# A new listed order of steps, with the rotating buffers given out by the list, in an attention and Mish kernel on one core

## The chip, the cores and the metric

The kernel runs on one core of one Trainium2 chip. The metric is the device time of one execution in microseconds (us): 923.94, the median of 3 runs, which lay between 922.16 and 925.21.

## What is computed

Eight batches of eight heads, 576 tokens each, of width 64: scores, a causal mask (a band of 32 keys for heads 0 to 3, every fourth of the last 128 keys for heads 4 to 7), a softmax and the product with v. The result, 4608 tokens of width 512, goes through a feed-forward network of 2048 channels with the Mish activation.

```python
scores = scale * np.matmul(q, k.transpose(0, 1, 3, 2))
mask_plain = (rel >= 0) & (rel < window)                  # window 32, dilation 4
mask_dil = (rel >= 0) & (rel < window * dilation) & (rel % dilation == 0)
scores = np.where(masks[None, :, :, :], scores, -1000000000.0)
scores = scores - np.max(scores, axis=-1, keepdims=True)
attn = np.exp(scores)
attn = attn / (np.sum(attn, axis=-1, keepdims=True) + 1e-09)
x = np.matmul(attn, v)                                    # then [4608, 512]
h = x @ w_in
sp = np.where(h > 20.0, h, np.log1p(np.exp(np.minimum(h, 20.0))))
out = (h * np.tanh(sp)) @ w_out
```

The two weights come as float64 and are unpacked on the chip.

## The kernel before, in words

**Units.** The work is cut into 16 units of 288 tokens (half a batch each). Units 0 to 3 do attention in float32, and turn x by products on TensorE. Units 4 to 7 use float16, and DMA transposes. Units 8 to 15 go in pairs 4 to 7; a pair's first layer is made by seven products per chunk of the channels, Strassen's way (`za` to `zg`, all products on L921), from sums of x (`zt`) and of the weights (`wf`, on POOL, L855 to L861), which lie in DRAM and are streamed in (`zl`, L879).

**Steps.** Each function of a unit is a generator in a few pieces, and each piece is a step with a two-letter name: `wl`, `wm`, `ww`, `ws`, `wp` load, measure, decode (DVE L394 to L397), scale and split a piece of the weights (ACT L351, ACT L406, DVE L409); `ld`, `lv` load q, k and v; `pr` prepares them (POOL L536 makes the low half of q); `sp` is the scores' product (PE L609, with the mask from PE L606 in units 0 to 3), `sc` reads them out of the bank (DVE L633, from unit 4 on), finds the maximum (DVE L639) and subtracts it (DVE L641); `ex` is the exponential (ACT L680; in the first units L667, straight from the bank), `tp` turns it (DVE L724, then the DMA of L727), `va` multiplies by v (PE L763; L757 in units 0 to 3), `ff` is a product of the first layer (PE L1009) and its Mish (ACT L1012; L931 for pairs), `gt` cuts Mish's result into float16 halves (ACT L1024, DVE L1026), `fo` is a product of the second layer (PE L1036), whose result ACT L1050 writes to a tile y that L1052 sends to DRAM, and `kw` is a number of products of zeros (`keep_warm`, PE L1065), whose results nobody reads.

**Order.** A text, `ORDER` (L40 to L179), lists all pieces of all units, 1 name for each piece. The loop at the end of the kernel goes through it and calls the next piece of the generator that is named. So the text sets the order of the instructions on every engine and every queue; nothing else does. What stands behind `=` in a name is the number of the buffer that the step is given:

```python
            name, _, at = name.partition("=")
            place[:] = [int(at)] if at else []
```

```python
        turns[name] = place[0] if place else (turns.get(name, -1) + 1) % len(tiles)
```

**Banks.** All products write to four PSUM tiles, `b0` to `b3` of 2 x 512 float32. A product for a bank waits until the engine that reads the bank's last result has read it. `keep_warm` is given `banks[3:]`, that is b3 alone.

**Rotating buffers.** In the kernel before, the raw weights (`raw`, 4 buffers), the transposed exponentials (`pp`, 2), `xs` (2), the scores (`sb`, 4), the results (`y`, 2) and Mish's results (`hm`, 3) are tiles of a pool with `bufs=N`: the pool gives them out in turn. `hm` is asked for in the same piece as the product that Mish will read (L1009, L921).

Of the kernel before, what the change touches and what calls it, by code (L numbers as in the profile page):

```python
# [10 lines left out]
F16 = mybir.dt.float16  # L11
BF16 = mybir.dt.bfloat16
F32 = mybir.dt.float32
# [39 lines left out]
tx1.0 tx1.0 tx1.3=0 va1.2 tx1.3 wp0.1.0 kw9=0 tx1.1=2 tx1.1 tx1.1 kw3=0 tx1.2=1 sp2.3=3 tx1.2 tx1.3 tx1.3 wl1.3.0
wl1.2.0 ww0.2.0 tx1.2 pr2=2 pr2 tx1.2 wm1.3.0 ww1.3.0 sc2.3 gt0.0=1 wp0.2.0 gt0.0 fs1 ff1.0=0 ww1.3.0 wl1.3.1 wm1.3.1
ff1.0 ff1.1=1 ff1.1 wp0.2.0 ff1.2=2 ff1.0 ff1.1 ff1.2 wl1.2.1 gt1.0=2 ff1.3=0 ff1.2 ww1.3.1 sp2.1=1 ld3 lv3 ww1.3.1
ex2.3 ws1.3=2 ff1.3 ws1.3 sc2.1 tp2.3=2 tp2.3 gt0.3 ff0.2=3 ff0.2 wm1.2.0 gt1.0 wm1.2.1 ff0.3=2 ex2.1 ff0.3 ww1.2.0
ff1.6=1 ww1.2.0 ff0.2 ff0.3 ff1.6 gt0.1=3 ww1.2.1 ww1.2.1 ff1.6 ff1.3 ws1.2=2 gt0.1 ff0.4=3 gt1.1=4 ff0.4 wp1.3.0
va2.3=1 tp2.1=0 tp2.1 ws1.2 ff0.4 sp3.0=2 gt1.1 sp3.1=0 va2.3 wp1.3.0 wp1.2.1 ff1.7=3 va2.3 wl1.0.1 ff1.7 wp1.2.1
ff1.4=1 ff1.7 gt1.3=5 sc3.0 wl1.0.0 wp1.2.0 sc3.1 gt1.3 ff1.5=3 wp1.3.1 ff1.4 ff1.5 sp3.3=2 va2.1=0 wp1.2.0 ff1.4
wm1.0.1 wp1.3.1 wl1.1.0 ff1.5 gt1.2=6 gt1.2 ff0.5=1 ww1.0.1 ff0.5 wm1.0.0 va2.1 fo1.2.0=3 ff0.5 ww1.0.0 gt0.2=7  # L60
ww1.0.0 fo1.2.1 fo1.2.2 ex3.1 va2.1 ws1.0=1 gt0.2 tp3.1=0 fo1.2.3 tp3.1 ws1.0 wm1.1.0 tp2.0=0 sp3.2=1 tp2.0 fo1.2.3
sp2.2=0 sc3.3 fo1.2.3 fo1.3.0 ld4 sc3.2 ex3.3 fo1.3.1 ww1.1.0 lv4 ww1.1.0 fo1.3.2 ex3.2 fo1.3.3 sc2.2 fo0.2.0=2 ex2.2
pr3 fo0.2.1 ww1.0.1 fo0.2.2 fo1.3.3 fs2 fo0.2.3 fo0.2.3 xa2.1=4 tx2.3=1 va2.0=0 fo0.2.3 tx2.3 tp2.2=3 fo0.3.0 fo1.3.3
tp2.2 va2.0 wp1.0.0 tx2.3 fo0.3.1 va2.0 wp1.0.0 ex3.0 fo0.3.2 fo0.3.3 fo0.3.3 wl1.1.1 xa2.0=0 fo0.3.3 tx2.0=3 va2.2=1
# [124 lines left out]
QB = 96  # L189
# [4 lines left out]
def attn_mish_ffn_kernel(  # L194
# [12 lines left out]
    P = 128  # L207
# [916 lines left out]
```

## Time and profile before

| | |
|---|---|
| median of the runs | 923.94 us |
| profiled execution, span | 926.8 us |
| mean granted clock of TensorE in it | 0.985 of full speed |
| TensorE products (PE) | 898.3 us busy, 97% |
| weight loads (PEld) | 725.8 us, 78% |
| VectorE (DVE) | 656.0 us, 71% |
| ScalarE (ACT) | 584.6 us, 63% |
| GpSimd (POOL) | 176.1 us, 19% |

The profile has one execution, from its first to its last instruction; its span is 2.9 us over the median of the runs. A row of a timeline says when a stretch of equal instructions began, how long it took, and in brackets how long the engine stood idle before it and what ended that. A row of the windows says how long each engine was busy in a stretch, and which clock TensorE was granted (1.00 is 2.4 GHz).

### The profile page before, as it was taken

How to read it: one execution, taken by the hardware profiler on the slowest of the kernel's cores; microseconds unless marked ns; L12 is line 12 of the kernel's file. 1: busy time of each engine (PE TensorE's matmuls, PEld its weight loads, DVE VectorE, ACT ScalarE, POOL GpSimd, SP SyncE). 2: the span in 40 equal slices, each digit the busy share in tenths (PEclk: the TensorE clock that was granted, in tenths of full speed). 3: DMA queues.
4: the chain of work that ended last, by engine and by line, in shares of the span. 5: the costliest groups of instructions: out<-in, count | busy, mean ns of one | idle time of the engine just before them, and what ended most of it. 6: DMA issues, size and time to landing. Idle time of an engine off the chain costs nothing.

```text
span 926.8 us, 21709 instructions
## 1 busy us (share of the span) xinstructions
PE 898.3 (97%) x9194; PEld 725.8 (78%) x9197; DVE 656.0 (71%) x905; ACT 584.6 (63%) x832; POOL 176.1 (19%) x196
## 2 busy tenths in 40 slices
PE   8899999999999989999889899999999999999998
PEld 7788888887787868887667777777877788887776
DVE  5787996678888687888868986997479965333400
ACT  2658775665685755768747677667687667535521
POOL 1000031114201160412430512131023500220000
PEclk9889999999999999999989999999999999999999
DMA  7844444130554365543656877865548655544300
GB/s 252 247 123 137 141 138 146 44 111 17 155 88 96 81 161 122 126 126 77 143 146 140 160 182 215 190 153 115 179 104 207 119 172 174 94 112 144 114 27 26
DMA packets 194194, 122.80 MB, mean 132 GB/s; under 512 B 139088, under 2 KB 182832, under 8 KB 194096
## 3 DMA queue, kind: packets, MB, share of 16 engines
q1 hardware_dynamic: 194096, 121.41, 50.9%
q8 instruction: 72, 1.18, 0.5%
q14 instruction: 26, 0.21, 0.1%
HBM read 78.38 MB, written 16.78 MB: 103 GB/s over the span
## 4 chain that ended last, share of the span: by engine, by line
PE 75%; DVE 10%; ACT 5%; DMA 4%; SPq 2%; issue 2%; POOL 2%; ACTq 0%; DVEq 0%
PE b L1036 30%; PE b L921 17%; PE b L1009 16%; PE b L609 3%; PE b L763 2%; PE b L757 2%; PE b L1065 2%; DVE sb L633 1%; DVE nm L639 1%; DVE k L539 1%; DMA raw<-in_w_in 1%; DVE g L1026 1%; DVE sb L641 1%; PE b L734 1%; DVE p L724 1%
## 5 line engine op out<-in xcount | busy, mean ns | idle before, releaser
L1036 PE MATMUL b<-g,w 128*128 128x288 f16 x3072 | 392.3, 288 | 0.0
L1036 PEld LDWEIGHTS <-w 128*128 128x128 f16 x3072 | 298.8, 98 | 77.0 <-issue 0.2
L1009 PE MATMUL b<-xf,w 128*128 128x288 f16 x1536 | 195.4, 287 | 1.6 <-ACT hm L1012 1.0
L1009 PEld LDWEIGHTS <-w 128*128 128x128 f16 x1536 | 149.7, 98 | 41.1 <-issue 2.1
L921 PEld LDWEIGHTS <-w 128*128 128x128 f16 x1344 | 130.9, 98 | 36.3 <-issue 2.9
L1026 DVE SCALAR_TENSOR_TENSOR g<-hm,sg,g 128x1152 f16<-128x1152 f32 x64 | 94.4, 1481 | 67.8 <-ACT g L1024 67.8
L921 PE MATMUL b<-xf,w 128*128 128x288 f16 x960 | 138.7, 286 | 2.9 <-ACT y L1050 1.5
L1050 ACT ACTIVATE y<-b,fo 128x288 f32<-128x288 f32 x60 | 43.3, 721 | 116.4 <-PE b L1036 93.7
L536 POOL TENSOR_TENSOR q<-qn,q 128x288 f16<-128x288 f32 (+1 forms) x36 | 55.6, 1573 | 158.1 <-ACT q L529 158.1
L1024 ACT ACTIVATE g<-hm,sg 128x1152 f16<-128x1152 f32 x64 | 80.3, 1254 | 2.6 <-PE b L1036 1.0
L1012 ACT ACTIVATE hm<-b,fs 128x576 f32<-128x576 f32 x64 | 45.9, 738 | 40.4 <-PE b L1009 24.9
L680 ACT ACTIVATE sb<-sb,ln_p 96x704 f32<-96x704 f32 (+3 forms) x48 | 42.5, 888 | 32.2 <-DVE sb L641 32.0
L931 ACT ACTIVATE hm<-hm,fs 128x576 f32<-128x576 f32 x48 | 36.4, 772 | 35.7 <-DVE hm L966 15.9
L724 DVE TENSOR_TENSOR p<-sb,p 96x704 f16<-96x704 f32 (+3 forms) x48 | 48.4, 1017 | 7.1 <-ACT p L722 6.9
L641 DVE TENSOR_TENSOR sb<-sb,nm 96x512 f32<-96x512 f32 (+4 forms) x60 | 50.9, 849 | 2.1
L639 DVE TENSOR_REDUCE nm<-sb 96x4 f32<-96x512 f32 (+4 forms) x60 | 44.9, 748 | 1.7
L855 POOL TENSOR_TENSOR hm<-w 128x1024 f32<-128x1024 f16 x8 | 18.8, 2353 | 139.5 <-DVE g L1026 139.5
L921 PE MATMUL b<-w,w 128*128 128x288 f16 x192 | 42.9, 286 | 0.0
L609 PE MATMUL b<-k,q 64*96 64x128 f16 (+3 forms) x1008 | 31.9, 210 | 8.5 <-POOL q L536 2.6
L609 PEld LDWEIGHTS <-q 64*72 64x72 f16 (+1 forms) x1008 | 26.8, 116 | 16.7 <-issue 10.1
L722 ACT CAST p<-sb 96x704 f16<-96x704 f32 (+3 forms) x48 | 37.8, 789 | 1.4 <-DMA pT<-p 0.3
L763 PEld LDWEIGHTS <-pT 128*128 128x128 f16 (+3 forms) x1008 | 35.4, 98 | 3.6 <-issue 1.7
(180 smaller groups left out, 1159.8 us busy)
## 6 DMA issues: line engine op xcount, KB each, us to landing
w<-wd SPq DMA_DIRECT2D x56, 512.0 KB
qn<-in_qT SPq DMA_DIRECT2D x16, 576.0 KB
out_T<-y SPq DMA_DIRECT2D x64, 144.0 KB
raw<-in_w_in SPq DMA_DIRECT2D x16, 512.0 KB
raw<-in_w_out SPq DMA_DIRECT2D x16, 512.0 KB
vn<-in_v SPq DMA_DIRECT2D x48, 128.0 KB
wd<-hm SPq DMA_DIRECT2D x32, 128.0 KB
knd<-in_kdT SPq DMA_DIRECT2D x16, 208.0 KB
```

Source lines behind the costliest of these rows:

```text
L536: nc.gpsimd.tensor_tensor(lo, x, hi, op=ALU.subtract)
L609: nc.tensor.matmul(o, q, k, start=start, stop=stop, skip_group_check=True)
L639: nc.vector.tensor_reduce(nm[:nq, :, j:j + n], x, axis=AX.X, op=ALU.max, negate=True)
L641: nc.vector.tensor_tensor(blocked(sb, c0, n, w), x, nm[:nq, :, j:j + n].unsqueeze(3).broadcast_to([nq, 2, n, w]), op=ALU.add)
L724: nc.vector.tensor_tensor(lo, src, hi, op=ALU.subtract)
L763: nc.tensor.matmul(avv[:, h, j], pp[:nk, c:c + P], vv[vi][:nk, j, hh, :], start=(i == 0), stop=(i == 2))
L921: nc.tensor.matmul(o[:, h, :HT], t[:, c, wi, h * P:(h + 1) * P], form_of(p, x, c, xi), skip_group_check=True, start=start and n == 0, stop ...
L1009: nc.tensor.matmul(ph[:, h, :HT], w1[j][c // WIDE][:, c % WIDE, wi, k * P:(k + 1) * P], x_of(d, xi, c), start=(n == 0), stop=(n == len(seq ...
L1012: nc.scalar.activation(d["m"][j][:, k0:k0 + 2], ph[:, :, :HT], AF.Mish, scale=d["fs"][:, j:j + 1])
L1024: nc.scalar.activation(g[:, 0], m, AF.Identity, scale=sg)
L1026: nc.vector.scalar_tensor_tensor(g[:, 1], m, sg, g[:, 0], ALU.mult, ALU.subtract)
L1036: nc.tensor.matmul(po[:, :HT], w2[:, e, j, wi, k * P:(k + 1) * P], d["g"][j][:, gi, k, :], start=(j == 0 and n == 0), stop=(j == NCH - 1 a ...
```

## The change

It replaces the list of the order by another with the same steps, except for the products of zeros: 251 for 451. All 251 are listed ahead of the first product of the first layer. In the list before, 375 are, 12 follow soon after, and 64 are spread over the rest of the list: 1, 30, 15, 15 and 3 at five places from unit 6's second layer on. `raw`, `pp`, `xs`, `sb`, `y` and `hm` become fixed lists of tiles, and the order's number says which one a step gets. `pp` is taken a piece later, and `hm` is taken in the piece that first writes it. `keep_warm` may use any of the four banks. The instructions are otherwise the same in number on each engine, but for ScalarE's loads of a function table: 52 for 40. Lines move by 7 or 8: L609, L1009, L1012, L1036 and L1050 become L616, L1017, L1020, L1044 and L1058.

```diff
 ORDER = """
...
-pr10 ld11 sp10.0=3 sc10.0 sp10.1=0 sp10.2=3 sc10.2 ex10.0 sc10.1 ex10.1 pr11 pr11 tp10.1=0 tp10.1 tp10.0=1 tp10.0
...
+pr10 va8.3 ff7.0=1 sp10.0=2 sc10.0=1 sp10.2=3 sp10.1=1 fo6.3.3=1 ex9.2 tp9.2=1 tp9.2 fo6.0.0=0 fo6.0.1 ex10.0 va9.3=2
...
+    raw4 = [early.tile([P, WIDE, CH], I64, name=f"raw{i}") for i in range(4)]
+    pps = [early.tile([P, 2, HT], F32, name=f"pp{i}") for i in range(2)]
+    xss = [early.tile([QB, 4, P], F32, name=f"xs{i}") for i in range(2)]
+    sbs = [pool.tile([QB, 2, NR * KD], F32, name=f"sb{i}") for i in range(4)]
+    ys = [pool.tile([P, HT], F32, name=f"y{i}") for i in range(2)]
...
-        t = early.tile([P, WIDE, CH], I64, name="raw", bufs=4)
+        t = take("raw", raw4)
...
-        sb = None if by_pe else pool.tile([QB, 2, NR * KD], F32, name="sb", bufs=4)
+        sb = None if by_pe else take("sb", sbs)
...
-        pp = d["p", pair] = early.tile([P, 2, HT], F32, name="pp", bufs=2)
-        yield
+        yield
+        pp = d["p", pair] = take("pp", pps)
...
+    hms = [pool.tile([P, FPC, HT], F32, name=f"hm{i}") for i in range(3)]
...
-            m[j] = pool.tile([P, FPC, HT], F32, name="hm", bufs=3)
+            m[j] = take("hm", hms)
...
         y = V[p]["Y", j] = take("b", banks)
+        product(p, j, "11", "11", y, True, False)
+        yield
         m = hm_of(2 * p, j)
-        product(p, j, "11", "11", y, True, False)
-        yield
...
-        if j not in d["m"]:
-            d["m"][j] = pool.tile([P, FPC, HT], F32, name="hm", bufs=3)
...
-        nc.scalar.activation(d["m"][j][:, k0:k0 + 2], ph[:, :, :HT], AF.Mish, scale=d["fs"][:, j:j + 1])
+        nc.scalar.activation(hm_of(u, j)[:, k0:k0 + 2], ph[:, :, :HT], AF.Mish, scale=d["fs"][:, j:j + 1])
...
-            y = pool.tile([P, HT], F32, name="y", bufs=2)
+            y = take("y", ys)
...
-        warm = take("w", banks[3:])
+        warm = take("w", banks)
```

Three places of the order follow, first of the kernel before, then of the change. The first is ScalarE at the start: the decoding of the first weights (L351), their split (L406) and the first exponentials of unit 0, read out of the banks (L667). `w` is a weight, `sb` the scores' tile.

```order
L351 ACTIVATE w100_104<-raw_159 128x1024
L272 ACTIVATE m_fb_96<-m_f_81 96x352
L406 ACTIVATE w100_104<-raw_159,ws1_330 128x2x512
L406 ACTIVATE w101_105<-raw_152,ws1_330 128x2x512
L351 ACTIVATE w130_110<-raw_418 128x1024
L667 ACTIVATE sb_430<-b1_73 72x2x288
L667 ACTIVATE sb_447<-b0_72 96x2x352
```

```order
L358 ACTIVATE w101_119<-raw1_77 128x1024
L279 ACTIVATE m_fb_110<-m_f_95 96x352
L358 ACTIVATE w130_124<-raw2_78 128x1024
L674 ACTIVATE sb0_84<-b0_72 96x2x352
L674 ACTIVATE sb1_85<-b1_73 96x2x352
L413 ACTIVATE w101_119<-raw1_77,ws1_398 128x2x512
L413 ACTIVATE w100_118<-raw0_76,ws1_398 128x2x512
```

The third decoding and the first two exponentials stand ahead of the split of the first weights now, not behind it. On SyncE's queue the load of the third piece of the weights stands ahead of the loads of v, not behind them.

The second place is TensorE at the first scores of unit 10 (behind each row shown follow more of its kind, each with its weight load).

```order
L1036 MATMUL b1_73<-g3_141,w2_112 128x288
...
L609 MATMUL b3_75<-k2_6350,q2_6348 96x128
...
L609 MATMUL b0_72<-k2_6350,q2_6348 96x128
...
L609 MATMUL b3_75<-k2_6350,q2_6348 72x72
...
L1009 MATMUL b2_74<-xf0_119,w100_104 128x288
```

```order
L1044 MATMUL b0_72<-g2_157,w2_126 128x288
...
L616 MATMUL b2_74<-k2_6146,q2_5988 96x128
...
L616 MATMUL b3_75<-k2_6146,q2_5988 72x72
...
L616 MATMUL b1_73<-k2_6146,q2_5988 96x128
...
L1044 MATMUL b0_72<-g1_156,w2_126 128x288
```

Before, the third scores take bank b3, which holds the first scores, with 18 small products between the two. In the change the three scores take three banks, and the product behind them a fourth.

The third place is ScalarE in the paired units: exponentials (L680, L687) and Mish (L931, L939) need different tables.

```order
L931 ACT_TABLE_LOAD
L931 ACTIVATE hm<-hm,fs 128x576 x3
L771 ACTIVATE den<-b_73,pf 72x8
L1024 ACTIVATE g_141<-hm,sg 128x1152
L771 ACTIVATE den<-b_72,pf 96x2x3
```

```order
L939 ACTIVATE hm_138<-b_74,fs 128x576
L729 CAST p_2316<-sb_86 72x8x104
L1032 ACTIVATE g_159<-hm_138,sg 128x1152
L687 ACT_TABLE_LOAD
L687 ACTIVATE sb_87<-sb_87,ln_p 72x832
L939 ACT_TABLE_LOAD
```

In the change an exponential stands alone between two Mish, with a table load on either side; in the piece of before the load is followed by Mish and gates, and no other load comes for over 80 rows.

## Rows read from the trace of the kernel before

**Rows 1.** The page, busy time of each engine; its chain of waits, by engine.

```profile
PE 898.3 (97%) x9194; PEld 725.8 (78%) x9197; DVE 656.0 (71%) x905; ACT 584.6 (63%) x832; POOL 176.1 (19%) x196
...
PE 75%; DVE 10%; ACT 5%; DMA 4%; SPq 2%; issue 2%; POOL 2%; ACTq 0%; DVEq 0%
```

**Rows 2.** TensorE by stretches: us, busy (products), granted clock, DMA share, GB/s.

```profile
0.00:25.00 25.00, 20.04 (x250) 1.00 0.81 262
25.00:75.00 50.00, 48.03 (x507) 0.86 0.57 169
75.00:200.00 125.00, 124.28 (x1211) 1.00 0.36 110
200.00:325.00 125.00, 124.77 (x1350) 1.00 0.42 98
325.00:350.00 25.00, 22.38 (x239) 0.93 0.63 165
350.00:425.00 75.00, 75.00 (x838) 1.00 0.49 117
425.00:550.00 125.00, 114.40 (x1242) 0.96 0.68 148
550.00:650.00 100.00, 97.94 (x1029) 1.00 0.67 165
650.00:900.00 250.00, 248.35 (x2358) 1.00 0.50 132
900.00:926.80 26.80, 23.10 (x189) 0.99 0.08 27
```

**Rows 3.** Chain of waits, pieces in order of time: start, us, what.

```profile
64.78 11.76 PE b L1009 x96
...
547.01 1.68 PE b L1065 x30
...
874.59 23.52 PE b L1036 x192
```

**Rows 4.** What TensorE waited for: us in total, times, longest.

```profile
PE b L606 <- ACT sb L667: 3.3, 1, 3.3
...
PE b L609 <- POOL q L536: 2.6, 1, 2.6
PE b L609 <- DVE sb L633: 2.5, 1, 2.5
```

**Rows 5.** Timeline of ScalarE, 16 to 25 us.

```profile
16.10 2.30 ACT L406 ACTIVATE w<-raw,ws 128x1024 f16<-128x1024 f32 x2 [5.50 <-DVE ws L374]
23.00 1.12 ACT L351 ACTIVATE w<-raw 128x1024 f32<-128x1024 f32 x1 [4.60 <-DMA raw<-in_w_in]
```

**Rows 6.** VectorE by stretches: us, busy (instructions), granted clock, DMA share, GB/s.

```profile
100.00:150.00 50.00, 48.60 (x73) 1.00 0.47 140
150.00:200.00 50.00, 30.24 (x62) 1.00 0.18 55
```

**Rows 7.** Timeline of TensorE at the first scores of unit 10.

```profile
482.11 0.64 PE L609 MATMUL b<-k,q 64*72 64x72 f16 x24 [2.53 <-DVE sb L633]
```

**Rows 8.** Timeline of POOL, 319 to 335 us.

```profile
319.73 3.23 POOL L855 TENSOR_TENSOR hm<-w 128x1024 f32<-128x1024 f16 x1 [38.79 <-DVE g L1026]
...
327.07 7.69 POOL L536 TENSOR_TENSOR q<-qn,q 128x288 f16<-128x288 f32 x3
```

**Rows 9.** ScalarE's table loads at one line: count, busy us, mean ns.

```profile
L680 ACT ACT_TABLE_LOAD x17 | 21.8, 1283 | 0.3
```

**Rows 10.** Timeline of ScalarE, 477 to 481 us.

```profile
477.44 1.28 ACT L1012 ACT_TABLE_LOAD   x1
478.73 0.74 ACT L1012 ACTIVATE hm<-b,fs 128x576 f32<-128x576 f32 x1
```

**Rows 11.** Chain of waits: a result on its way to DRAM.

```profile
525.16 3.82 DMA out_T<-y
```

More of the change, by code (lines that the diff above doesn't have):

```diff
@@ new lines @@
+ff7.1=1 xw10.1=2 sc10.2=0 ff7.1 ff7.1 pr11 zt4.0.1 xw9.1=0 va9.3 va9.2=3 va9.2 wf3.1=2 va9.2 fo6.1.0 ff7.2=1 wf3.1
+ff7.2 ex10.1 ff7.7=2 pr10 ff7.3=3 ff7.3 ff7.7 tp10.1=1 fo6.1.1 tp10.1 zt4.1.0=0 zt4.1.0=3 zt4.1.0 zt4.1.1=4 gt7.0=1
+gt7.0 fo6.1.2 zt4.1.3=1 ex10.2 fo6.0.3 ff7.3=1 ff7.2 lv11 pr11 pr11 ff7.7 zt4.1.1=0 zt4.1.1 gt7.3=3 gt7.3 gt7.1=4
+tp10.0=1 gt7.1 tp10.2=0 fo6.1.3 fo6.1.3=1 xw10.0=1 tp10.2 pr11=3 fo7.0.0=1 wf3.1=0 pr11 pr11 va10.0=2 tp10.1=0 pr11
+sp10.3=0 fo7.0.1 sc10.3=3 va10.0 va10.0 tp10.2=1 zt4.1.0 wf3.1 wf3.1 fo6.1.3 va10.1=3 va10.1 zt4.1.2=5 va10.1 ex10.3
@@ new lines @@
+gt11.1=7 zf5.1 gt10.1=0 fo9.3.3 gt11.1 zd5.2 tp13.0=0 va13.0=3 zl5.9=2 zb5.2=1 zd5.2 ex13.2 zc5.2 zc5.2 zg5.2 zl5.10=0
+pr14 zl5.11=1 ze5.2 va13.0 za5.3=0 tp13.3=1 tp12.3=0 gt10.1 zl5.12=2 ze5.2 zf5.2 zg5.2 zc5.3=2 va13.0 zt6.0.0=3
+zt6.0.0=0 za5.3=2 zc5.3 zt6.0.0 fo9.1.3 zf5.2 gt10.2=2 gt10.2 va12.2=3 zc5.3 va12.3=1 va12.3 zl5.13=0 zt6.0.0 zt6.1.0=0
+zd5.3 zd5.3=0 zb5.3=2 zb5.3 ze5.3 pr14 zg5.3 va12.3 tp13.2=0 zg5.2 ze5.3 pr14=1 pr14 tp13.3 tp13.3=1 zt6.0.1=2
+zt6.0.1=1 va12.2 pr14 zt6.0.1 zt6.0.2=1 zt6.0.1 zf5.3 zf5.3 va12.2 gt10.3=1 zg5.3 ze5.2 gt11.2=3 fo10.2.0=1 fo10.2.1
@@ new lines @@
+zc6.0=1 sp15.3=0 zf6.0 ex15.1 va14.1 zc6.0 tp15.1=0 tp15.1 zl6.4=0 va14.1 fs12 ze6.0 za6.1=1 zg6.0 sc15.3=3 sp15.2=3
+zc6.0 zc6.1=0 zf6.0 gt12.0=4 gt12.0 tp15.0=1 za6.1=0 zc6.1 zb6.1=2 zl6.5=2 zd6.1 zl6.6=1 zb6.1=2 fo11.1.3 zg6.1
+sc15.2=0 zd6.1 va14.0=0 zg6.1 zl6.8=0 tp14.2=1 va14.0 zg6.1 ze6.1 zc6.2=3 gt13.0=0 tp14.2 ze6.1 zl6.7=2 gt13.0 ze6.1
+gt13.1=2 zc6.1 zf6.1 va14.0 gt13.1 za6.2=2 zf6.1 zb6.2=0 za6.2=1 zd6.2 zb6.2=2 gt12.1=1 pr15 zc6.2 va15.0=1 va15.0
+fo11.3.3 tp15.1=0 zc6.2 zl6.9=1 zg6.2 zd6.2 zg6.2 va15.1=3 va15.1 va15.0 ze6.2 ze6.2 zl6.11=2 zb6.3=0 zg6.2 zl6.10=0
@@ new lines @@
+fo13.1.1 fo13.2.3=0 zl7.3=1 zt7.0.2 fo13.1.2 zt7.0.2 fo13.0.3 fo13.1.3 va15.2=2 va15.2 zl7.1=0 xw15.1=0 va15.2
+zt7.1.3=1 zt7.1.0=1 va15.3=1 va15.3 fo13.3.0 fo13.3.1 va15.3 fo13.3.2 fo13.3.3 zt7.1.0 gt12.3=6 gt12.3 zl7.0=2
+fo12.0.0=2 fo12.0.1 fo12.0.2 fo13.2.3 zt7.1.0 zc7.0=1 zt7.1.1=1 zt7.1.1=0 fo13.3.3=1 zt7.1.1 zt7.1.1 fo12.0.3
+fo12.0.3=0 fo12.0.3 zt7.1.2=5 zt7.1.3=1 zt7.1.2=0 zt7.1.3 zt7.1.3 za7.0=0 zt7.1.2 fo13.1.3=0 fo13.1.3 fo12.1.0 za7.0=2
+zt7.1.2 fo12.1.1 fo12.1.2 zc7.0 fo13.3.3 fo12.1.3 fo12.2.0=3 fo12.2.1 zd7.0 zd7.0=1 fo12.2.2 zl7.2=0 zb7.0=1 fo12.2.3
@@ new lines @@
+fo12.2.3 zb7.3=0 zd7.3 zg7.3 zd7.3 zl7.13=2 ze7.3 fo14.2.0=3 gt14.2 ze7.3 zf7.3 zf7.3 gt14.3=3 fo14.2.1 ze7.3 fo14.2.2
+fo14.0.1 fo14.0.2 gt14.3 fo14.2.3 fo14.2.3=0 fo15.0.0=2 zg7.3 fo15.2.0=0 fo15.2.1 fo14.2.3 fo15.0.1 zg7.3 gt15.3=6
+fo14.0.3 fo14.0.3=1 fo15.2.2 fo14.1.0 fo14.1.1 fo14.1.2 fo14.0.3 gt15.3 fo15.2.3 fo15.2.3=0 fo15.2.3 fo14.3.0 fo15.3.0
+fo15.0.2 fo15.3.1 fo15.0.3 fo15.0.3=1 fo15.0.3 fo14.3.1 fo15.1.0 fo15.3.2 fo15.3.3 fo15.3.3=0 fo15.3.3 fo15.1.1
+fo14.3.2 fo14.3.3 fo14.3.3=1 fo14.3.3 fo15.1.2 fo15.1.3 fo15.1.3=0 fo15.1.3 fo14.1.3 fo14.1.3=1 fo14.1.3
@@ L665, in exps @@
             yield
-            sb = d["sb", pair] = pool.tile([QB, 2, NR * KD], F32, name="sb", bufs=4)
+            sb = d["sb", pair] = take("sb", sbs)
             nc.scalar.activation(sb[:nq, :, :width], pt[:nq, :, :width], AF.Exp, scale=1.0 / math.sqrt(D))
@@ L774, in values @@
         if d["direct"]:
-            xs = d["xs", pair] = early.tile([QB, 4, P], F32, name="xs", bufs=2)
+            xs = d["xs", pair] = take("x", xss)
         else:
@@ L853, in w_forms @@
         t = w1[j][cp]
-        x = pool.tile([P, FPC, HT], F32, name="hm", bufs=3).rearrange("p a b -> p (a b)")[:, :2 * CH].rearrange("p (c n) -> p c n", c=2)
+        x = take("hm", hms).rearrange("p a b -> p (a b)")[:, :2 * CH].rearrange("p (c n) -> p c n", c=2)
         nc.gpsimd.tensor_tensor(x, t[:, :, 0], t[:, :, 1], op=ALU.add)
@@ L862, in w_forms @@
         yield
-        o = pool.tile([P, FPC, HT], F32, name="hm", bufs=3).rearrange("p a b -> p (a b)")[:, :2 * CH].bitcast(F16)
+        o = take("hm", hms).rearrange("p a b -> p (a b)")[:, :2 * CH].bitcast(F16)
         o = o.rearrange("p (i c n) -> p i c n", i=2, c=2)
@@ L976, in s_p3 @@
     def s_p3(p, j):
-        w, m = V[p]["W", j], hm_of(2 * p + 1, j)
+        w = V[p]["W", j]
         product(p, j, "S4", "22", w, False, True)
         yield
+        m = hm_of(2 * p + 1, j)
         nc.vector.tensor_tensor(m[:, :2], w[:, :, :HT], m[:, :2], op=ALU.add)
```

262 lines of the change are left out of this document (120 added, 142 removed).

## The prediction

> **What bounds the kernel now.** I read the busy times and the chain of waits first, then TensorE by stretches, then what TensorE waited for, and at the worst waits the timelines. TensorE is busy for 97% of the span and holds 75% of the chain; VectorE comes next, with 71% and 10% [rows 1]. So the bound is TensorE, and what a new order can give back is only the time in which TensorE does nothing useful. That is of three kinds.
>
> *Idle.* The stretches add up to 28.5 us (926.8 less 898.3). They are not spread evenly: 5.0 us in the first 25, 2.0 in the next 50, 2.6 in 325 to 350, 10.6 in 425 to 550, 2.1 in 550 to 650, 1.7 in 650 to 900 and 3.7 in the end [rows 2]. From 75 to 325 and from 350 to 425 there is nearly none.
>
> *A lower clock.* The mean granted clock is 0.86 in 25 to 75, 0.93 in 325 to 350 and 0.96 in 425 to 550 [rows 2]: 0.14 x 50 = 7.0 us, 0.07 x 25 = 1.75 us and 0.04 x 125 = 5.0 us lost. Each such stretch holds idle time; a wait costs its length and then some more.
>
> *Zeros.* Thirty products of zeros take 1.68 us, 56 ns each [rows 3]; the 451 are 25 us.
>
> What is left is useful work, and the change touches none of it. A product of 288 columns goes through every 122.5 ns (192 in 23.52 us [rows 3]), and the 5952 of them are 729 us before as after.
>
> **The change, part by part.** The sum is made against the profiled execution's 926.8 us; the median of the runs is 2.9 us lower, so 2.9 comes off at the end.
>
> *The start.* Up to 75 us TensorE loses 6.9 us of idle, 387 x 56 ns = 21.7 us of zeros (375 ahead of the first product of the first layer, 12 soon after) and 7.0 us of clock: 35.6 in all. Fewer zeros by themselves give nothing there: a zero that goes leaves an idle slot if VectorE isn't ready. So I counted both lists, with the durations of this trace for each line: how much VectorE work is listed up to each point, and how much useful TensorE work. The greatest lead of VectorE's work is 33.2 us before, close to the 35.6 lost, and 27.3 us in the change; ahead of the first product of the first layer stand 49.5 us of VectorE work before and 41.0 now. The difference of the leads, 5.9 us, is what the start can give. On ScalarE it fits the first piece of the order: the third decoding stood behind the split of the first weights and waited 4.6 us for its data at 23.00, and the exponentials behind it kept TensorE for 3.3 us [rows 4, 5]. Now these exponentials stand ahead of the split, and the weights' third piece is loaded ahead of v. I take **-6**; the ends are 0 (another chain is as long) and -12 (the 5.0 us of idle in the first 25 us and all of the clock's 7.0).
>
> *The 64 zeros of the later list* go: 64 x 56 ns = **-3.6** us, if TensorE has work there. If not, it stands idle instead and the gain is 0; that end is in the range.
>
> *425 to 550 us: banks.* Here 10.6 us of idle and 5.0 of clock are lost. The wait of 2.53 us at 482.11 ended when VectorE had read the first scores of unit 10 out of bank b3 [rows 7]: the 24 products behind it are the third scores, which the list puts into b3 with 18 small products in between (the second piece of the order). Counting TensorE's work between the last product for an old tenant of a bank and the first for a new one, the list of before has 14 products with less than 1 us and 22 with less than 1.6; the change has none and 9, all of 1.47 to 1.50 us. Those under 1.3 us in before belong to ten steps, of which eight show a wait in the trace; of the eight from 1.3 to 1.6 one does. In the change's second piece the three scores have three banks and the product behind them a fourth. So most of these waits lose their cause, and with them the clock that follows. I take two thirds of 15.6, **-10.4**; the ends are 0 and -15.6. What is late next is the VectorE work itself, which is why I don't take all: the most that the list puts beside 25 us of TensorE work is 28.2 us before (four such places over 25) and 24.9 in the change.
>
> *325 to 350 us: POOL.* TensorE waited 2.6 us for q [rows 4]. POOL made q from 327.07 on, behind a sum of weights that had waited 38.79 us for a tile of Mish's results that a gate had yet to read [rows 8]. In the change the same sum stands ahead of the same q, but the list gives it the tile, and `hm` is taken at the first write, so a tile is held for a shorter time. Idle and clock are 4.4 us there; I take half, **-2.2**, ends 0 and -4.4.
>
> *550 to 900 us*: 3.7 us of idle in small waits for tiles and banks of the same kinds; half, **-1.9**, ends 0 and -3.7.
>
> *Twelve more table loads on ScalarE.* A load takes 1283 ns [rows 9], so 15.4 us more on an engine that is idle for 342 of 926.8 us [rows 1]. The cover is that idle time and the distance in the list between an exponential and the products that need it: counted as above, the shortest from a scores' product to its use by v is 21.0 us of TensorE work in the change, 17.3 before. I cost it at **0**; without the cover it is +15.4.
> The row of a load shows 1.28 us at 477.44 and the next activation at 478.73, at once [rows 10]. The Trainium skill, "ScalarE: Activation LUTs", section "What ACT_TABLE_LOAD costs", puts about 1.38 us of draining on top, 2.66 us for a switch, and its section on table sets has functions of one set grouped, which speaks against the change. By the page twelve loads would be an estimated 31.9 us of ScalarE; the trace shows no drain behind the load, and the measurement decides.
>
> *The end.* The last result and its way to DRAM, 3.7 us after TensorE's last product, stay. The buffers that are now given by number cost no instruction.
>
> Sum: -6 - 3.6 - 10.4 - 2.2 - 1.9 = -24.1; 926.8 - 24.1 = 902.7, and less 2.9: **899.8 us**.
>
> **The rivals.**
>
> *VectorE stays the bound (914.3).* After its peak VectorE's lead falls to 13 to 17 us by 150 us of TensorE's work in the list of before, while in the change it stays at 20 to 27 up to 165. In 100 to 150 us VectorE was busy for 48.6 of 50, without hurting TensorE, and then had 19.8 us free [rows 6]. If TensorE must wait where the lead is larger (23.5 against 15 at the middle, 8.5 us) and so gives back the start's 6, the time is 899.8 + 8.5 + 6 = 914.3. For it speaks how full VectorE is there, against it that TensorE did not wait in that stretch at all.
>
> *New waits in the place of the old (914.3).* The waits from 325 on are replaced by others of like size: the 14.5 us of the three later terms don't come, 899.8 + 14.5 = 914.3. The nearest candidate is y: two tiles, whose way to DRAM took 3.82 us in one case [rows 11]; the change lists 6 of 62 writes with less TensorE work than that since the tile's last sending, the shortest 1.5 us. Against it: a write to y holds a bank, but only for the rest of that distance.
>
> *All of it works (884).* The start gives 12, the later stretches all of 15.6 + 4.4 + 3.7 = 23.7, the zeros 3.6: 923.9 - 39.3 = 884.6.
>
> *Slower: ScalarE's table loads decide (929.8).* In the change's third piece an exponential stands alone between two Mish, so two loads lie in front of a Mish that gates and products of the second layer wait for. If ScalarE is the late engine in the paired units, each of the twelve loads is on the path, +15.4, and the three later terms don't come; the start and the zeros do: 923.9 - 9.6 + 15.4 = 929.7. It decides from the point at which ScalarE has less than 1.3 us to spare at such a place. Against it: ScalarE is busy for 63% alone [rows 1].
>
> **How the numbers follow.** Forecast 52%, its own range 891 to 908 (from 8 us more of the terms' ends to 8 less). VectorE 15%, new waits 14%, all of it 12%, slower 7%. The predicted time is the forecast's, 900. The range holds 8 in 10 if it takes in the forecast, the upper two rivals with some spread to 919, and the gain of all down to 884. About 0.3%, 2.8 us, can be told from no change, so faster is under 921.2 and slower over 926.7. The forecast, all of it, and most of the two at 914.3 are faster: 0.87; the rest of those two is within: 0.06; slower 0.07.
>
> **What would show it.** Right: the granted clock from 425 to 550 us over 0.98, and idle there under 5 us; no wait over 1 us of L616 for VectorE reading a bank; the first product of the first layer (64.78 us before [rows 3]) about 6 us earlier or with less idle behind it. The loads' cost is nil if none of TensorE's waits for L1020 or L939 is over 1 us. Wrong: VectorE busy for over 97% from 75 to 190 us with TensorE idle beside it; rows of waits for y or for ScalarE among the longest; the stretch from 25 to 75 us still at a clock of 0.86.

## The result, and the profile after

The changed kernel takes **896.31 us** (median of 4 runs, 895.06 to 898.11), the kernel before 923.05 (4 runs, 918.67 to 925.21): 0.9712 of the time, with a 95% interval of 0.9681 to 0.9742. The forecast was 900, and faster. The gain is 26.7 us by the medians. The two profiled executions lie 33.4 us apart (926.8 and 893.4), because that of before is a long one; this is taken up below.

TensorE by the stretches of [rows 2], in the changed kernel (us, busy and products, granted clock, DMA share, GB/s):

```profile
0.00:25.00 25.00, 23.78 (x309) 1.00 0.86 269
25.00:75.00 50.00, 48.28 (x491) 0.97 0.57 168
75.00:200.00 125.00, 121.11 (x1161) 0.99 0.40 126
200.00:325.00 125.00, 123.81 (x1354) 1.00 0.53 122
325.00:350.00 25.00, 25.00 (x269) 1.00 0.28 72
...
425.00:550.00 125.00, 124.37 (x1322) 1.00 0.72 172
550.00:650.00 100.00, 99.16 (x1053) 1.00 0.67 163
650.00:866.00 216.00, 214.82 (x2043) 1.00 0.49 125
```

What is lost in a stretch is its idle time and what its clock lacks, as in the prediction:

| stretch, us | lost before [rows 2] | lost after |
|---|---|---|
| 0 to 75, without zeros | 6.9 + 7.0 | 2.9 + 1.5 |
| 75 to 200 | 0.7 | 3.9 + 1.2 |
| 200 to 325 | 0.2 | 1.2 |
| 325 to 350 | 2.6 + 1.8 | 0 |
| 425 to 550 | 10.6 + 5.0 | 0.6 |
| 550 on, without the last stretch | 3.7 | 2.0 |

The zeros, which the table leaves out, take 33.1 us of TensorE in the trace of before and 16.8 us in that of the change. From 325 us on nearly nothing is lost now; from 75 to 325 more than before. The first product of the first layer starts at 49.14 us, 15.6 earlier than the 64.78 of [rows 3] (12.1 earlier than in another execution of the list of before, where it starts at 61.24), and the zeros ahead of it are 251 instead of 375. Its row in the timeline of TensorE:

```profile
49.14 1.03 PE L1017 MATMUL b<-xf,w 128*128 128x288 f16 x7
```

What TensorE waits for, in all (us, times, longest), against [rows 4]: the three long waits there are gone. The longest now end with ScalarE's L1058, which reads a result out of its bank and writes it to a tile y: 2.0 us at most. What held L1058 up is taken up below.

```profile
PE b L1044 <- ACT y L1058: 3.2, 2, 2.0
PE b L1073 <- DVE zeros L1068: 1.0, 1, 1.0
PE b L770 <- DMA pT<-p: 1.0, 2, 0.6
```

ScalarE at the start, against [rows 5]: the third decoding runs at 16.15 instead of 23.00, the exponential stands ahead of the split, and the split comes at 20.51.

```profile
16.15 1.12 ACT L358 ACTIVATE w<-raw 128x1024 f32<-128x1024 f32 x1 [5.67 <-DMA raw<-in_w_in]
17.32 0.75 ACT L674 ACTIVATE sb<-b 96x704 f32<-96x704 f32 x1
...
20.51 2.38 ACT L413 ACTIVATE w<-raw,ws 128x1024 f16<-128x1024 f32 x2
```

### The profile page after: what moved, and what is told of

Read it like the earlier page. It is cut to its first block, busy times and chain, and to the rows that moved or that the text cites. A ratio compares the mean times of both kernels' runs of the same rounds, so it can differ in the third digit from the quotient of the medians.

```text
span 893.4 us, 21281 instructions
## 1 busy us (share of the span) xinstructions
PE 879.0 (98%) x8997; PEld 704.5 (79%) x8997; DVE 647.8 (73%) x905; ACT 593.2 (66%) x844; POOL 170.8 (19%) x196
## 4 chain that ended last, share of the span: by engine, by line
PE 67%; DVE 10%; issue 9%; ACT 5%; DMA 4%; POOL 4%; SPq 2%; DVEq 0%; ACTq 0%; POOLq 0%
PE b L1044 29%; PE b L929 18%; PE b L1017 13%; PE b L770 3%; PE b L616 3%; DVE g L1034 1%; DVE m L319 1%; DMA raw<-in_w_out 1%; DVE nm L646 1%; DVE sb L648 1%; POOL q L543 1%; SPq L463 1%; SPq L465 1%; DVE p L731 1%; DVE w L914 1%
## 5 line engine op out<-in xcount | busy, mean ns | idle before, releaser
L1044 PE MATMUL b<-g,w 128*128 128x288 f16 x3072 | 392.9, 287 | 3.6 <-ACT y L1058 3.2
L1044 PEld LDWEIGHTS <-w 128*128 128x128 f16 x3072 | 296.5, 98 | 79.4 <-issue 4.4
L1017 PE MATMUL b<-xf,w 128*128 128x288 f16 x1536 | 196.1, 286 | 0.2 <-DVE xs L788 0.2
L1017 PEld LDWEIGHTS <-w 128*128 128x128 f16 x1536 | 148.5, 98 | 38.1 <-DVE xs L788 0.3
L1034 DVE SCALAR_TENSOR_TENSOR g<-hm,sg,g 128x1152 f16<-128x1152 f32 x64 | 91.6, 1435 | 25.5 <-ACT g L1032 25.2
L1058 ACT ACTIVATE y<-b,fo 128x288 f32<-128x288 f32 x60 | 43.3, 722 | 92.8 <-PE b L1044 69.4
L1020 ACT ACTIVATE hm<-b,fs 128x576 f32<-128x576 f32 x64 | 46.2, 737 | 39.4 <-PE b L1017 36.9
L543 POOL TENSOR_TENSOR q<-qn,q 128x288 f16<-128x288 f32 (+1 forms) x36 | 38.8, 1106 | 157.2 <-ACT q L536 157.2
L687 ACT ACTIVATE sb<-sb,ln_p 96x704 f32<-96x704 f32 (+3 forms) x48 | 42.5, 892 | 19.6 <-DVE sb L648 19.2
L648 DVE TENSOR_TENSOR sb<-sb,nm 96x512 f32<-96x512 f32 (+4 forms) x60 | 49.1, 818 | 2.1
L863 POOL TENSOR_TENSOR hm<-w 128x1024 f32<-128x1024 f16 x8 | 23.3, 2908 | 123.6 <-DVE g L1034 116.6
L939 ACT ACTIVATE hm<-hm,fs 128x576 f32<-128x576 f32 x48 | 36.3, 769 | 12.3 <-DVE hm L975 8.0
L975 DVE TENSOR_TENSOR hm<-b,hm 128x576 f32<-128x576 f32 x16 | 12.1, 757 | 30.9 <-PE b L929 25.6
L616 PEld LDWEIGHTS <-q 64*72 64x72 f16 (+1 forms) x1008 | 26.2, 115 | 10.3 <-issue 9.9
```

Source lines behind the costliest of these rows:

```text
L543: nc.gpsimd.tensor_tensor(lo, x, hi, op=ALU.subtract)
L616: nc.tensor.matmul(o, q, k, start=start, stop=stop, skip_group_check=True)
L648: nc.vector.tensor_tensor(blocked(sb, c0, n, w), x, nm[:nq, :, j:j + n].unsqueeze(3).broadcast_to([nq, 2, n, w]), op=ALU.add)
L1017: nc.tensor.matmul(ph[:, h, :HT], w1[j][c // WIDE][:, c % WIDE, wi, k * P:(k + 1) * P], x_of(d, xi, c), start=(n == 0), stop=(n == len(seq ...
L1020: nc.scalar.activation(hm_of(u, j)[:, k0:k0 + 2], ph[:, :, :HT], AF.Mish, scale=d["fs"][:, j:j + 1])
L1034: nc.vector.scalar_tensor_tensor(g[:, 1], m, sg, g[:, 0], ALU.mult, ALU.subtract)
```

## The experiments

Each kernel was timed against the kernel before on its own chip; the median of before lay between 922.9 and 923.6 in these comparisons. Its run-to-run spread (917.85 to 928.71 over all) is wider than that of the changed kernel, so a difference of 2 us is not told from none.

### The code alone, and the two halves of the list

First the change's code with the list of before, step by step; the numbers for the tiles that are now fixed are added. Two places of the list, against the changed kernel:

```diff
 ORDER = """
-wl0.0.0=0 wm0.0.0=0 wl0.0.1=1 ld0 ww0.0.0 kw16=0 kw7=0 kw16=0
+xa1.0=0 wl0.0.1=0 wm0.0.1=0 ww0.0.1 ww0.0.1 wl0.0.0=1 wm0.0.0=0 ww0.0.0
...
-pr10 va8.3 ff7.0=1 sp10.0=2 sc10.0=1 ex9.2 sp10.2=3 sp10.1=1 fo6.3.3=1
+ld11 sp10.0=3 sc10.0=2 sp10.1=0 sp10.2=3 sc10.2=0 ex10.0 sc10.1=1 ex10.1
```

> The code of the change with the order of before, step by step, and its 451 zeros; the buffers that are now fixed lists are given the tile that has been free longest, as rotation would. If the order is what brings the gain, the time is that of before: 921 to 926. If taking the tiles late and by number matters by itself, the 330 us stall (4.4 us with its clock) and some of the waits for Mish's tiles go: 916 to 919.

Measured: 922.96, ratio 0.9994 (0.9973 to 1.0015). The code does nothing by itself; the whole gain is the order's. Its profile, of the same order as before, is 921.3 us long and shows what varies in the start (the row of [rows 2] has a clock of 0.86, which is 7.0 us lost; here it is 0.91, 4.5 us):

```profile
25.00:75.00 50.00, 48.15 (x519) 0.91 0.63 186
...
425.00:550.00 125.00, 115.09 (x1266) 0.97 0.66 152
```

So part of the 33.4 us between the two profiles is the start of that one execution, and the stretch from 425 to 550 us loses 13.7 us in it, not 15.6. Then two mixed lists, cut at the first product of the first layer.

The first has the new list up to there and then the order of before for all steps that are left, the second the other way round. The seam of each, against the changed kernel:

```diff
 wl0.0.0=0 wm0.0.0=0 wl0.0.1=1 ld0 ww0.0.0 kw16=0 kw7=0 kw16=0
...
-ws0.1=1 sc1.2=1 ex1.2 ff0.6=3 ws0.1 fs0 ff0.0=0 ff0.7=2
+wp0.1.0 sc1.2=1 ex1.2 wp0.2.1 wp0.2.1 fs0 ff0.0=3 ff0.0 ff0.0=0 ff0.6=0 ff0.7=2
```

```diff
-wl0.0.0=0 wm0.0.0=0 wl0.0.1=1 ld0 ww0.0.0 kw16=0 kw7=0 kw16=0
+xa1.0=0 wl0.0.1=0 wm0.0.1=0 ww0.0.1 ww0.0.1 wl0.0.0=1 wm0.0.0=0 ww0.0.0
...
-wm0.1.1=0 xa2.0=3 ex1.1 ws0.2 ww0.1.1 ex2.0 ff0.0=0 ff0.0
+ws0.2 wp0.2.1 wp0.2.1 fs0 ww0.2.0 xa2.0=3 ff0.0=0 ff0.0
```

> The changed kernel's code, with the new list up to the first product of the first layer and then the steps that are left in the order of the list before (with its 76 zeros from there on; 327 in all). The traces put the start's worth at 13.6 us up to 75 us, of which 4.6 come back as waits up to 200: by that 914 (911 to 917). If what VectorE has still to do behind the shorter start decides, the gain is given back in the old rest as well: 920 to 924. If the new start is worth more with the old rest, whose VectorE steps stand farther apart up to 200 us: 909.

> The changed kernel's code, with the list of before up to the first product of the first layer and then the new list's order of what is left (375 zeros, none behind). The new rest is worth 25 us by the traces, the new start 9: by that 905 (902 to 909). If the two are not independent, because the old start leaves less VectorE work for the stretch up to 200 us, 898 to 901.

Old start and new rest: 906.58, ratio 0.9813 (0.978 to 0.9846). That was expected (905): the new rest is worth 16.5 us, and the new start the 10.3 from there to 896.31. New start and old rest: 925.12, ratio 1.0035 (1.0014 to 1.0056), a miss by 11 us. This mix was badly made. What the old list has ahead of its first product of the first layer, and the new one behind, comes right behind the cut, so that TensorE waits for the weights that are made there:

```profile
PE b L1017 <- DVE wm L376: 4.5, 1, 4.5
PE b L369 <- DVE w L401: 3.8, 2, 3.2
```

(The second halves of x of units 0 and 1 also share a tile in it, so that a part of these units' result is not the reference's.) In its profile 11.2 us are idle from 25 to 75 us, where the changed kernel has 1.7. So the 10.3 us of the new start hold with the new rest behind it; what the start would be worth with the old rest and a clean seam isn't shown.

### Banks

Three kernels in which no step moves, and only bank numbers differ. Of the first two one place of the list is shown, unit 10's scores.

```diff
-ld11 sp10.0=3 sc10.0 sp10.1=0 sp10.2=3 sc10.2
+ld11 sp10.0=0 sc10.0 sp10.1=2 sp10.2=3 sc10.2
```

> The kernel before, no step moved; from 130 us of TensorE's work on each product is given the bank whose last product lies longest back (167 bank numbers differ; zeros may use any bank). Of the ten steps that come under 1.3 us behind a bank's former tenant, five lose their neighbour, among them the 2.53 us wait at unit 10's third scores; the others have no free bank to go to. If quick reuse of banks is what costs time in 425 to 550 us, some 4.5 us of idle time and 2 of clock go: 917 (915 to 920). If the waits only show that VectorE is late there, they move to the next product: 921 to 925.

Measured: 950.36, ratio 1.0293 (1.0264 to 1.0321). Not 6 us less but 27 more. Waits of TensorE in it:

```profile
PE b L1007 <- DVE g L779: 6.7, 2, 5.4
PE b L761 <- DVE sb L631: 5.3, 5, 1.8
PE b L1034 <- DVE sb L631: 3.7, 1, 3.7
```

The distance from the last product, on which the prediction's term was counted, is no measure. The results of `va` are read by VectorE (L779, L781 before) only when ScalarE has written the sum (`den`): a bank whose last product is old can still be unread. The second kernel takes the bank that had really been read longest ago:

```diff
-ld11 sp10.0=3 sc10.0 sp10.1=0 sp10.2=3 sc10.2
+ld11 sp10.0=1 sc10.0 sp10.1=0 sp10.2=2 sc10.2
```

> The kernel before, no step moved; this time each product from 130 us of TensorE's work on is given the bank whose last read (on ScalarE or VectorE) ended first in the trace of before, 90 numbers differ. In that trace 17 products started within 0.3 us after their bank had been read; with this choice 13 would have, and unit 10's third scores (2.53 us), unit 11's third (0.86) and the first product of pair 4 (1.54) are among those that would not. If the time of the reading is what decides, some 5 us of idle time and 1.4 of clock go: 917 (915 to 919). If bank numbers can't help without moving steps, 921 to 925.

Measured: 923.53, ratio 1.0004 (0.9978 to 1.003): nothing. Unit 10's third scores have a bank that is free, and now wait for the low half of k instead; the product behind them waits for the bank:

```profile
477.96 0.54 PE L607 MATMUL b<-k,q 64*72 64x72 f16 x20 [1.36 <-DVE k L537]
478.82 4.77 PE L1007 MATMUL b<-xf,w 128*128 128x288 f16 x24 [0.32 <-DVE sb L631]
```

The third kernel makes banks worse in the changed kernel, at eight steps (the sixteen numbers that differ are shown, without the steps between them):

```diff
-ff6.2=3 sp9.1=2 sp9.0=2 va8.1=1 ff6.1=2 sp9.2=1 ff6.7=1 va9.1=2
+ff6.2=2 sp9.1=3 sp9.0=3 va8.1=3 ff6.1=1 sp9.2=3 ff6.7=3 va9.1=3
-va8.2=2 ff7.5=3 va8.3=1 pr10=3 ff7.0=3 sp10.0=2 va9.2=3 va10.2=3
+va8.2=3 ff7.5=1 va8.3=2 pr10=1 ff7.0=1 sp10.0=1 va9.2=1 va10.2=1
```

> The changed kernel, no step moved; 16 bank numbers differ, so that eight steps between 350 and 470 us of TensorE's work come 0 to 0.7 us behind the last product of their bank's former tenant. If quick reuse of banks is the cause, eight waits of 0.7 to 2.5 us appear, 6 to 14 us with the clock that follows: 903 to 911. If VectorE's and ScalarE's readiness decides and not the bank, the time stays at 895 to 899.

Measured: 909.70, ratio 0.9859 (0.983 to 0.9887), 13.4 us over the changed kernel. Each of the eight steps shows its wait, two of them here:

```profile
401.20 0.72 PE L770 MATMUL b<-vh,pT 128*128 128x65 f16 x18 [1.11 <-DVE sb L640]
403.94 0.30 PE L1017 MATMUL b<-xf,w 128*128 128x288 f16 x1 [2.02 <-DVE g L788]
```

So the banks can cost as much as the term said. But in the kernel before, neither of the two other choices of banks gave it back: at unit 10's scores a free bank only laid bare the next wait, the one for k.

### Why they were late: two steps of the list before

```diff
-wf1.0 wf1.1 wf1.1 fo3.1.2
+wf1.0 fo3.1.2
...
-fo4.2.2 fo3.3.3 pr7 pr7 pr7 ld8
+fo4.2.2 fo3.3.3 pr7 pr7 pr7 wf1.1 wf1.1 ld8
...
-sc9.1 pr9 pr9 ff6.3 ff6.3
+sc9.1 pr9 pr9 ld10 lv10 ff6.3 ff6.3
...
-ex9.2 tp9.2=0 tp9.2 ld10 pr10 pr10 lv10
+ex9.2 tp9.2=0 tp9.2 pr10 pr10
```

> The kernel before with two moves in the list. Unit 10's loads of q, k and v (one step each) stand behind the last piece of unit 9's preparation, 32 us of TensorE's work earlier, instead of 17 us ahead of unit 10's first scores; and the two first pieces of the weights' sum that held POOL at 320 us stand behind unit 7's low half of q instead of ahead of it. The trace of before shows the loads issued at 452.5 behind the turning of the exponentials on SyncE's queue, landed at 460.4, VectorE waiting with its maximum for them, and behind that the read of the bank for which TensorE waited 3.1 us at 459.9; unit 10's scores follow late. If this chain is the cause in 425 to 490 us and POOL's order at 330, then 9 and 4 us go: 910 (908 to 914). If ScalarE and VectorE are late anyhow, the waits stay: 920 to 924; the stretches tell which of the two moves works.

Measured: 917.48, ratio 0.9926 (0.9901 to 0.9951): 6 us less, half of what was expected. POOL makes unit 7's low half of q at 307.82 now, 19 us earlier than in [rows 8], ahead of the weights' sum, and the stretch from 325 to 350 loses 0.4 us instead of 4.4:

```profile
307.82 3.75 POOL L534 TENSOR_TENSOR q<-qn,q 128x288 f16<-128x288 f32 x3 [30.35 <-ACT q L527]
318.46 2.64 POOL L853 TENSOR_TENSOR hm<-w 128x1024 f32<-128x1024 f16 x1 [6.89 <-DVE g L1024]
```

```profile
325.00:350.00 25.00, 24.57 (x296) 1.00 0.65 157
...
425.00:550.00 125.00, 117.45 (x1297) 0.99 0.64 147
```

In 425 to 550 us some 8.8 us are lost instead of 15.6. The loads of unit 10 go out at 414.34 instead of 452.5. The wait at 460 us that they were moved for shrinks from 3.1 to 1.8 us, but unit 10's third scores wait as long as in [rows 7]. The cause is one step further on. Behind the first scores VectorE first makes k's low half for the other heads, for 2.67 us, and reads the bank after that:

```profile
467.38 2.67 DVE L537 SCALAR_TENSOR_TENSOR k<-knd,s,k 128x576 f16<-128x576 f32 x1
469.98 0.94 DVE L631 SCALAR_TENSOR_TENSOR sb<-b,sc,m_r 96x704 f32<-96x704 f32 x1
```

The new list has the same 2.67 us on VectorE, but 48 products of the second layer stand ahead of the scores on TensorE; the three scores then run in one piece, each in a bank of its own:

```profile
446.56 6.04 PE L1044 MATMUL b<-g,w 128*128 128x288 f16 x48
450.06 2.67 DVE L546 SCALAR_TENSOR_TENSOR k<-knd,s,k 128x576 f16<-128x576 f32 x1
452.54 1.75 PE L616 MATMUL b<-k,q 64*96 64x128 f16 x60
```

The order on POOL is shown by this as the cause at 330 us. The load is a smaller one: of the 6.1 us, some 4.0 are gained at 330, which leaves about 2 for it. (By the stretch it looks like more, but 425 to 550 us lost 13.7 in the other execution of the list of before.) The rest of the 16.5 us is many small waits of this kind; which step takes away which was not tried.

### Products of zeros

```diff
-fo6.2.3 kw1=0 fo6.3.0
+fo6.2.3 fo6.3.0
...
-va10.3 kw16=0 kw14=0 pr12=3
+va10.3 pr12=3
...
-gt9.1 kw15=0 zf4.1
+gt9.1 zf4.1
...
-ze5.1 kw15=0 zf5.1
+ze5.1 zf5.1
...
-pr14 kw3=0 pr14=3
+pr14 pr14=3
```

> The kernel before without the last 64 products of zeros. By the prediction's term 3.6 us go: 919.4. If TensorE stands idle in their place, because what they stand before isn't ready, nothing: 922 to 924; if idle time there also lowers the clock, 925 to 927.

Measured: 923.33, ratio 1.0002 (0.9974 to 1.003). The zeros stood where TensorE would have been idle; leaving them out gives idle time. Two of the five places show it, the first row from the kernel before, the others from this one. The single zero (`kw1`) itself waited 3.10 us for bank b3; without it the next product waits 1.64 us for its own bank. Where 30 zeros stood, for 1.68 us in [rows 3], the next product now waits 1.55 us:

```profile
463.02 0.29 PE L1065 MATMUL b<-zeros 128*128 128x128 f16 x1 [3.10 <-DVE g L781]
...
459.60 6.04 PE L1033 MATMUL b<-g,w 128*128 128x288 f16 x48 [1.64 <-ACT y L1047]
541.71 0.18 PE L318 MATMUL b<-m,ones 128*128 128x6 bf16 x1 [1.55 <-DVE m L309]
```

The other test takes all zeros out of the changed kernel:

```diff
-ww0.0.0 kw16=0 kw7=0 kw16=0 kw16=0 kw16=0 kw16=0 kw16=0 kw16=0 kw16=0 kw16=0 kw16=0 kw15=0 sp0.0=0
+ww0.0.0 sp0.0=0
...
```

> The changed kernel without any product of zeros. The 251 take 16.8 us of TensorE in its trace, all ahead of 75 us, and by the account of the start they stand where TensorE would be idle anyway, so that the time hardly moves through their going: 895 to 898. What they may do is to keep the granted clock up: if the useful products of the first 75 us then run at half speed for some 10 us of work, 5 to 10 us are lost: 901 to 906. If zeros stood in the way of useful products, 890 to 894.

Measured: 900.27 (895.42 to 903.72), ratio 0.9759 (0.971 to 0.9808): 4.0 us over the changed kernel by the medians, with intervals that overlap, so that the size is not settled. The profile shows where such a loss can come from. TensorE, idle in the first 12.5 us, is granted less than with the zeros in the third and fourth stretch (0.86 and 0.68; with the zeros 1.00 and 0.86):

```profile
0.00:12.50 12.50, 1.80 (x12) 1.00 0.86 296
12.50:25.00 12.50, 11.78 (x89) 1.00 0.98 285
25.00:37.50 12.50, 9.98 (x97) 0.86 0.66 227
37.50:50.00 12.50, 10.48 (x79) 0.68 0.76 227
```

The first product of the first layer comes at 53.09 us there, 3.95 later than with the zeros. In three other executions with the new start and its zeros the third stretch has 1.00 each time, the fourth 1.00, 1.00 and 0.64; so only the third is told apart.

### ScalarE's table loads

```diff
         act_mish(p, j, m[:, :2], m[:, :2])
+        if p < 7:
+            nc.scalar.activation(spare, ident[:1, :1], AF.Exp)
```

> The changed kernel with one exponential of a single element (its result is read by nothing) behind twelve Mish of the pairs 4 to 6, which makes 74 table loads of 52: 22 x 1283 ns = 28.2 us more on ScalarE, over twice what the change added. If the loads are hidden, 896 to 899. If they are on the path, 924 (or a good part of it, over 910, if half of them are).

Measured: 917.87, ratio 0.9951 (0.9927 to 0.9976): 21.6 us over the changed kernel, of 28.2 added (and 2.4 for the twelve exponentials, 0.20 us each). In the units of the pairs TensorE waits for Mish and for the copies that stand behind it on ScalarE, where in the changed kernel it waited for Mish for 0.4 us in all:

```profile
PE b L929 <- ACT hm L948: 4.5, 3, 2.8
PE b L929 <- ACT hm L972: 3.9, 2, 3.2
PE b L929 <- ACT hm L941: 3.0, 3, 2.2
```

The opposite test takes the loads away:

```diff
-            nc.scalar.activation(x, x, AF.Exp, bias=ln_p[:nq])
+            nc.scalar.activation(x, x, AF.Relu, bias=ln_p[:nq])
```

> The changed kernel with Relu in the place of the exponential in units 4 to 15, so that the softmax there isn't the reference's: Relu needs no table of its own, and the table loads fall from 52 to 8, 56 us less on ScalarE. If the loads are hidden in the changed kernel: 893 to 897. If the twelve that the change added are on the path, at least 12 of 44 in proportion: 885 or less.

> The kernel before with the same replacement (units 4 to 15 with Relu, not the reference's softmax): 6 loads for 40, 44 us less on ScalarE. If ScalarE's lateness, with its loads between 424 and 445 us in the chain of waits, makes the waits of the middle, 10 us or more go: 905 to 913. If the order of the loads and reads makes them whatever ScalarE does: 919 to 924.

Measured: 894.51 for the changed kernel so altered (893.95 to 894.92; ratio to before 0.9685, 0.967 to 0.9699) and 921.84 for that of before (ratio 0.9983, 0.9965 to 1.0). Forty-four loads fewer, 56 us of ScalarE, give 1.8 us by the medians; thirty-four fewer give 1.7, both at the edge of what can be told. The loads are hidden in both kernels, so ScalarE's lateness did not make the waits of before either. The loads of the changed kernel, 22 of the 52 in front of an exponential, with 0.4 us of idle time ahead of them in all, against [rows 9]:

```profile
L687 ACT ACT_TABLE_LOAD x22 | 28.2, 1283 | 0.4
```

## Why the prediction was right, and where not

**The size.** Forecast -24.1 us, measured -26.7. The parts are less even than the sum, and that it came so near is in part luck: the start gave 4 us more than its term, the 64 zeros 3.6 less, 425 to 550 us some 3 to 5 more by the traces, and 75 to 325 us, which had no term, loses 5.4 us more than before.

**The start, -6: right in kind, too small.** It is 10.3 by the mixed list (with the new rest). The wait of the first exponentials and the late third decoding went as the rows of ScalarE show. The count of VectorE's lead over TensorE gave 5.9; the bound of 12 was nearer. The clock accounts for part of what was missed: in 25 to 75 us it is 0.97 now and 1.00, 1.00 and 0.90 in three other executions with this start and its zeros; in the eight with the old start it is 0.86 to 0.95. The zeros of the first 85 us took 28.6 us of TensorE in the trace of before, not the 21.7 that 56 ns each make, and take 16.8 now. The prediction set the saved zeros at nothing there; the runs without the late ones and without any agree with that reasoning, since neither is faster.

**The 64 zeros, -3.6: wrong.** Leaving them out of the kernel before gives 0 (2.4 us less at most, by the interval). The end that the prediction named (idle time in their place) is what happens.

**425 to 550 us, -10.4 for banks: too small, and the reason only half.** The stretch lost 15.6 (13.7 in the other execution) and loses 0.6. But other numbers for the banks alone gave nothing, or 27 us more, and the list's moves were needed. The step that failed is "most of these waits lose their cause": the cause is that the reading engine is late, as VectorE with k's low half at unit 10, and a bank's quick return is where that shows; with another bank the same product waited for k itself. The count by the distance from the last product was the wrong measure. That the bank numbers must fit the order is nevertheless true: 16 wrong ones cost 13.4 us.

**POOL at 330, -2.2: right in kind, half the size.** The stretch loses nothing now, 4.4 us less. Moving the sum's two pieces behind q in the old list takes the wait away as well. The new list does it in another way: the sum still stands ahead of q, as the prediction read, but so much earlier that it waits 6.96 us for its tile, not 38.79, and q is made at 299.94:

```profile
265.87 4.29 POOL L863 TENSOR_TENSOR hm<-w 128x1024 f32<-128x1024 f16 x1 [6.96 <-DVE hm L875]
...
299.94 2.94 POOL L543 TENSOR_TENSOR q<-qn,q 128x288 f16<-128x288 f32 x3 [25.52 <-ACT q L536]
```

That `hm` is taken later was not the reason by itself: the code alone gave nothing.

**550 to 900 us, -1.9: right.** The stretches lost 3.7 and lose 2.0.

**Table loads, 0: right, at the places of the new list.** Taking 44 away gives 1.8 us, so the twelve added ones cost hardly anything. But 22 more, around an exponential put right behind a Mish, cost nearly a microsecond each. The slower rival needed ScalarE to have under 1.3 us to spare at such places; it has more than that at the places that the new list chose, and not at the twelve of the experiment. The Trainium skill, "ScalarE: Activation LUTs", section "Table sets: the hidden batching unit", says to do all calls of one table set before those of the next. The changed kernel does so less than before and is faster; the kernel with more loads shows the rule at work. The drain that the section "What ACT_TABLE_LOAD costs" counts on top does not appear behind a load here either, where two stand 1.52 us apart:

```profile
523.32 1.28 ACT L966 ACT_TABLE_LOAD   x1
524.62 0.20 ACT L966 ACTIVATE spare<-ident 1x1 f32<-1x1 f32 x1
524.84 1.28 ACT L941 ACT_TABLE_LOAD   x1
526.13 0.78 ACT L941 ACTIVATE hm<-hm,fs 128x576 f32<-128x576 f32 x1
```

**VectorE as the bound up to 200 us: the stretch was right, the cause was not.** From 75 to 200 us 5.1 us are lost for 0.7 before, 4.4 given back, where the rival named it, against 8.5 that it priced. But VectorE is busy for 91.0 of the 115 us from 75 to 190, 79%, as it was before; the rival's sign was over 97%. The longest wait of the stretch, 2.03 us, with a clock of 0.89 in the 12.5 us from 175 on, ends a chain in which VectorE itself stands idle for 4.00 us:

```profile
165.60 1.80 POOL L704 MEMSET p<- 96x2048 f16 x1 [39.87 <-DVE w L416]
...
171.52 1.35 DVE L319 TENSOR_REDUCE m<-qn 128x1 bf16<-128x1152 f32 x1 [4.00 <-POOL m L489]
172.79 0.20 DVE L1050 TENSOR_SCALAR fo<-h_o,f 128x1 f32<-128x1 f32 x1
...
173.07 0.50 ACT L1058 ACTIVATE y<-b,fo 128x288 f32<-128x288 f32 x1 [7.41 <-DVE fo L1050]
...
173.63 2.28 PE L1044 MATMUL b<-g,w 128*128 128x288 f16 x12 [2.03 <-ACT y L1058]
```

POOL clears new tiles (L704, L706) and the m of L489 behind them, VectorE's reduction L319 waits for that m, the factor `fo` is listed behind the reduction, and ScalarE can't read the bank without `fo`. The kernel with the old start and the new rest has the same wait (2.02 us at 186.17), so it comes with the new rest and is not the price of the shorter start. That moving `fo` or the clearing would take it away was not tried.

**New waits for y: in name only.** The 3.2 us of L1058 are two waits of 2.03 and 1.18 us. The first is the one above; at the second, at 698.56, ScalarE was busy with other work from 693.48 until it came to L1058. Neither is a wait for a y on its way to DRAM, which the rival priced.

**The 2.9 us between profile and median.** The profile of before holds a lower clock in its start (0.86) than the seven other executions with the same start (0.90 to 0.95). It made the start look worse to mend than it mostly is; measured against the medians the sum was still closer than its parts.

## What to carry to other kernels

When an in-order engine waits for a buffer, look at what the engine that frees it does just before: moving that work, or the load it needs, helps where another buffer number does not, and a number that looks free in the list can cost more than the wait. Idle time that is filled with dummy work is not a gain to be had by leaving the dummy work out. Work on an engine with slack is free only at the places that have slack: the same table load cost next to nothing in 44 places and nearly a microsecond in others.

## Not expected

Bank numbers alone, with every instruction in its place, moved the time of the kernel before by 27 us. And POOL's three subtractions for unit 7's q took 7.69 us in the kernel before and 3.75 at their new place in the run with two moves, with VectorE busy beside them for 74% of that time in the one and 66% in the other; over the whole kernel the 36 of this line take 55.6 us before and 38.8 in the changed kernel:

```profile
L543 POOL TENSOR_TENSOR q<-qn,q 128x288 f16<-128x288 f32 (+1 forms) x36 | 38.8, 1106 | 157.2 <-ACT q L536 157.2
```

What makes them longer was not tried.
